# Expert sums weighed on VectorE, and added to the outputs by DMAs, in an attention and Sinkhorn-routing kernel

## The chip, the cores and the metric

The kernel runs on one core of a Trainium2 chip. The metric is device time in microseconds (us) of one execution; less is better. Three executions before the change took 891.78, 892.31 and 892.71 us, median 892.31. The profiled execution is a further one, with its own time.

A core has five engines with queues of their own. TensorE (PE in the profile) multiplies matrices, VectorE (DVE) and ScalarE (ACT) work element by element, GpSimd (POOL) can do so too and writes the descriptors of the DMAs that it issues, and SyncE (SP) here only issues DMAs. An engine runs its queue strictly in order: an instruction that waits for a semaphore holds everything behind it.

## The reference

Two blocks, one after the other. The first is a polynomial attention: queries and keys are sketched by two small projections, whose 8 x 8 outer products are the features; its result is a matrix x of 4352 tokens by 128. The second is a mixture of 8 experts, in which every token goes through every expert:

```
logits = x @ w_gate                      # 4352 x 8
P = exp(logits - max)
8 times: P /= row sums; P /= column sums; P *= N / E
for e in range(8):
    h = maximum(x @ w1[e], 0)            # 128 -> 1024
    out += P[:, e:e+1] * (h @ w2[e])     # 1024 -> 128
```

All of it is in 32-bit floats. Nearly all arithmetic is in the experts. P is positive, so a weight may be applied to x before the first product, or to the expert's result after the second.

## The kernel before, in words

Tokens lie along the free axis of the tiles and the 128 channels on the partitions: `xT` holds x transposed. The kernel avoids multiplications by fast matrix schemes: an expert's second product is computed from sums and differences of blocks of h and of w2, seven block products in place of eight, or twenty for a larger scheme, and the output is put together from four banks of PSUM by further sums.

The experts' work is cut into *groups* of tokens (list `groups`, lines 713 to 722) and *items*, one for each expert of a group. The routing weights P exist only after attention and routing are finished. To keep TensorE busy meanwhile, expert 0 is computed for all tokens and expert 1 for the first 1280, without weights, and the results are kept in SBUF: `kept[0]` (128 x 4352) and `kept[1]` (128 x 1280). These kept sums are weighed later, when P is there.

The late groups are weighted ones. Five of them have 768 tokens in three tiles of 256 columns (their first tokens are 1280, 512, 2048, 2816 and 3584; the first of them is called `PLAIN`), one has 512 tokens in two tiles and comes last. The five take experts 1 to 7, the group at 512 and the last one 2 to 7. For each of them x is multiplied by the expert's weights before the first product.

All but the first two items of the five groups are done by `middle` (line 1258). It is a planner by hand: `add(time, job)` puts jobs on a list with a planned time, the list is sorted, and the jobs are emitted in that order. So planned times only set the order in each engine's queue. A *block* is half an item, `PERIOD` = 8.83 us long (line 1255); there are 64. An item starts at t and takes two blocks, q = 0 and 1. In every block there are three slots for less urgent work (`EASE`, at 11.93, 13.85 and 16.87 from a block's start, applied one period later): `at_ease` (line 1363) moves what is in the list `soon` out and then emits a single job of the list `later`.

What the change touches:

- `weigh_half` (825): multiplies half of x (384 columns) by an expert's weights into `xe`, two items ahead. The first half takes x as it is; the second takes a negated copy of x, which `negate` (818) has ScalarE write once for each group into the free end of `hb` (`spare`).
- `copy_half` (836) and `join_halves` (843): ScalarE copies the halves to `de`, and four adding DMAs on GpSimd's queue form their sums in `de` and `xe`. The third of the four, `de[:, 0] += de[:, 1]`, waits until the first two have landed. `join_halves` is planned at t + `WEIGH` + 1, that is t + 14.49.
- `weigh_kept` (853): for group g, the i-th call loads the weights of expert i from DRAM (`pT`, broadcast over the partitions, on SP) at t + 5 and has GpSimd multiply the kept sums by them, 256 columns at a time (`weigh`, 796), with 3.7 us of plan between the pieces. One item later `plus` adds `kept[1]` to `kept[0]` by a DMA, where there are two, and for the last group `less` has GpSimd subtract one half of the columns from the other. Over all groups these are 22 multiplies of 128 x 256 and one subtraction.
- `part_of_twenty` (990): when one of a group's four banks is finished, ScalarE copies it out (`own[k]`; `evacuate`, planned at `EMPTY` in the group's last block) and a row of additions and subtractions on VectorE is put on `later`, which build the output y, three thirds of 256 columns. The first ones are: `y[:, 0]` from bank 0; `y[:, 1]` from banks 1 and 0; then, with bank 2, three operations on `y[:, 2]` and line 1011, `y[lower, 1] -= own[1][lower, 1]`, where `lower` is partitions 0 to 63. Near the end of the row three additions add the weighed kept sums to the thirds (line 1040); then the thirds are transposed and stored. The next group's first blocks carry this row, and after the fifth group the closing stage (`steps`, 1543) does.

A queue rule matters for the prediction: `keep_in_program_order` keeps GpSimd's and SP's instructions in the order in which they are emitted.

Of the kernel before, what the change touches and what calls it, by code (L numbers as in the profile page):

```python
# [10 lines left out]
F32 = mybir.dt.float32  # L11
# [39 lines left out]
def kernel(  # L51
# [736 lines left out]
    def weights_of(e, lo, n, tag):  # L788
        if tag == "pb":
            pb = spare[:, 6 * NT3 + 2 * HALF:9 * NT3 + 2 * HALF][:, 0:n]  # L790
        else:
            pb = pools[0].tile([P, 3 * NT3], F32, tag=tag, name=tag, bufs=3)[:, 0:n]
        tc.keep_in_program_order(nc.sync.dma_start(out=pb, in_=pT[e:e + 1, lo:lo + n].to_broadcast([P, n])))
        return pb

    def weigh(out, x, pb):
        tc.keep_in_program_order(nc.gpsimd.tensor_tensor(out, x, pb, op=Alu.mult))
# [15 lines left out]
    weights, turned_off = {}, {}  # L813
# [4 lines left out]
    def negate(g):  # L818

        lo = groups[g][0]  # L820
        c = 6 * NT3 + HALF * (g % 2)
        x = turned_off[g] = spare[:, c:c + HALF]
        nc.scalar.activation(out=x, in_=xT[:, lo + HALF:lo + 2 * HALF], func=Act.Copy, scale=-1.0)

    def weigh_half(j, i, engine):

        g = items[j][0]
        lo = groups[g][0]
        if i == 0:
            sources[j] = [pools[0].tile([P, 2, HALF], F32, tag="xe", name="xe", bufs=3)]  # L830
        x = turned_off[g] if i else xT[:, lo:lo + HALF]
        ins = engine.tensor_tensor(sources[j][0][:, i], x, weights[j][:, HALF * i:HALF * (i + 1)], op=Alu.mult)
        if engine is nc.gpsimd:
            tc.keep_in_program_order(ins)
# [18 lines left out]
    def weigh_kept(g, i):  # L853

        lo, n, t, es, _ = groups[g]
        ys = [kept[e][:, lo:lo + n * t] for e in range(es[0])]
        if i < len(ys):
            pb = []

            def piece(c):  # L860
                if not c:
                    pb.append(weights_of(i, lo, n * t, "pb"))
                sl = slice(c, c + NT3)
                weigh(ys[i][:, sl], ys[i][:, sl], pb[0][:, sl])

            return [lambda c=c: piece(c) for c in range(0, n * t, NT3)]

        def plus(y):
            tc.keep_in_program_order(nc.gpsimd.dma_start(out=ys[0], in_=y, accum_op=Alu.add))

        def less():
            k1, k2 = ys[0][upper, 0:n], ys[0][upper, n:2 * n]
            tc.keep_in_program_order(nc.gpsimd.tensor_tensor(k1, k1, k2, op=Alu.subtract))

        return [lambda y=y: plus(y) for y in ys[1:]] + [less] * (t == 2)
# [114 lines left out]
    def part_of_twenty(g, k):  # L990
# [7 lines left out]
        def do(out, a, b, off=False):  # L998
            at_leisure(lambda: nc.vector.tensor_tensor(out, a, b, op=Alu.subtract if off else Alu.add))
# [12 lines left out]
        if all(i in own for i in range(4)):  # L1012
# [26 lines left out]
            for i in range(3):  # L1039
                do(y[:, i], y[:, i], kept[0][:, lo + NT3 * i:lo + NT3 * (i + 1)])  # L1040
# [217 lines left out]
    def middle():  # L1258
# [114 lines left out]
        for n, k in enumerate(ks):  # L1373
# [5 lines left out]
            if q == 0:  # L1379
# [19 lines left out]
                if 1 + late <= es.index(e) <= es[0] + 1 + late:  # L1399
                    for i, do in enumerate(weigh_kept(g, es.index(e) - 1 - late)):  # L1400
                        add(t + 5 + 3.7 * i, do)
                if g == len(groups) - 2 and 3 <= es.index(e) <= 5:
                    for i, do in enumerate(weigh_kept(len(groups) - 1, es.index(e) - 3)):
                        add(t + 5 + 3.7 * i, do)
            ahead = j + 2 + q
            if new_of(ahead):
                if q:
                    add(t + WEIGH - 9, fetch_weights, ahead)
                    if items[ahead - 1][0] != items[ahead][0]:
                        add(t + WEIGH, negate, items[ahead][0])  # L1410
                add(t + WEIGH, weigh_half, ahead, 1 - q, nc.vector)
# [35 lines left out]
        add(WEIGH - 0.6, weigh_half, first_new + 2, 0, nc.vector)  # L1447
# [60 lines left out]
    def beside(j, c):  # L1508
# [17 lines left out]
        if new_of(j + 1) or new_of(j + 2):  # L1526
            for do, *a in PREPARE.get(c if new_of(j + 1) else c - 16, ()):
# [4 lines left out]
    PREPARE = {-14: ((fetch_weights, first_new),), -9: ((weigh_half, first_new, 0, nc.vector),),  # L1532
               -8: ((negate, PLAIN), (copy_half, first_new, 0)), -7: ((weigh_half, first_new, 1, nc.vector),),
               -6: ((copy_half, first_new, 1),), -5: ((join_halves, first_new),),
               0: ((fetch_weights, first_new + 1), (raw_second, first_new, "ws"), (first_weights, first_new)),
               4: ((weigh_half, first_new + 1, 0, nc.vector),), 5: ((weigh_half, first_new + 1, 1, nc.vector),),
# [194 lines left out]
```

## Time and profile before

| | |
|---|---|
| median of three runs | 892.31 us |
| profiled execution, its own time | 892.21 us |
| span of the profiled execution | 890.4 us |
| TensorE busy | 880.1 us, 99% |
| VectorE busy | 788.3 us, 89% |
| ScalarE busy | 561.7 us, 63% |
| GpSimd busy | 180.9 us, 20% |
| mean granted TensorE clock | 0.999 |

The profile gives one execution. Its groups of instructions (a row is: code line, engine, operation, output and input tiles, shape, count, then busy time in us, mean duration in ns, and the idle time before them) and its timeline (start in us, duration in us, engine, line, operation, count; in brackets the engine's idle time before it and what ended that) are used below. A source view of one line gives the shortest, median and longest duration in ns, and the first and last start in us. A windows row gives a stretch, its length, and each engine's busy time in it with its count of instructions. A DMA row gives queue, count, size in KB and the median time in us from issue to landing. Two or three equal VectorE instructions in a row are one timeline row with their joint duration. Where VectorE's instructions follow each other closely, their durations overlap a little.

### The profile page before, as it was taken

Reading aid. Unit: us, or ns where it says so; the run is one execution under the profiler, and the core shown is the slowest. Engines: PE = TensorE matmul, PEld = TensorE weight load, DVE = VectorE, ACT = ScalarE, POOL = GpSimd, SP = SyncE. Lnnn points to the kernel's source line nnn. Section 1 sums busy time; section 2 is a strip of 40 time slices with the busy share of each in tenths; the row PEclk is TensorE's granted clock in tenths of the full one; section 3 lists DMA queues with packets and bytes.
Section 4 is the critical chain, followed back from the end, with each engine's and each line's share of the span. In section 5 each row is a group of like instructions: output and inputs, shape, how many; then the busy total and the mean of one; then the engine's idle time right before and its main releaser. Section 6 shows DMA issues by size and latency. Waiting matters only on the chain.

```text
span 890.4 us, 28221 instructions
## 1 busy us (share of the span) xinstructions
PE 880.1 (99%) x11586; PEld 615.3 (69%) x11586; DVE 788.3 (89%) x1595; ACT 561.7 (63%) x1288; POOL 180.9 (20%) x242
## 2 busy tenths in 40 slices
PE   8999999999999999999999999999999999999997
PEld 6777544555677777676777777777777786666665
DVE  7678788889799999999999998999989999987865
ACT  3355477666577676676767666766667676655543
POOL 3121123012133213321222211321122213100000
PEclk9999999999999999999999999999999999999999
DMA  9996359658989777767776687567676775750340
GB/s 257 304 282 228 95 106 215 165 151 184 292 249 237 233 209 239 205 183 187 215 238 160 179 213 227 170 186 211 197 194 186 233 210 152 173 176 28 116 103 13
DMA packets 92721, 169.13 MB, mean 190 GB/s; under 512 B 28704, under 2 KB 65008, under 8 KB 87744
## 3 DMA queue, kind: packets, MB, share of 16 engines
q1 hardware_dynamic: 73264, 137.68, 49.2%
q0 software_dynamic: 18096, 29.49, 18.7%
q8 instruction: 91, 1.49, 0.7%
q10 hardware_dynamic: 1232, 0.16, 0.1%
q14 instruction: 38, 0.31, 0.1%
HBM read 123.60 MB, written 25.08 MB: 167 GB/s over the span
## 4 chain that ended last, share of the span: by engine, by line
PE 92%; DVE 5%; ACT 1%; issue 1%; DMA 1%; SPq 0%; DVEq 0%; ACTq 0%
PE s L1492 39%; PE a L1275 34%; PE a L1091 14%; PE a L423 1%; DVE hb L1177 1%; PE a L538 1%; DVE hx L1177 1%; DMA kx<-in_k_dram 1%; PE a L390 0%; DVE hb L1110 0%; PE s L452 0%; PE a L502 0%; DVE a L1312 0%; DVE hx L1312 0%; PE s L468 0%
## 5 line engine op out<-in xcount | busy, mean ns | idle before, releaser
L1275 PE MATMUL a<-xe,w 64*64 64x384 f32 x2052 | 397.4, 483 | 0.0
L1492 PE MATMUL s<-hb,ws 64*64 64x256 f32 (+4 forms) x2904 | 375.8, 384 | 1.6 <-DVE hb L1110 0.9
L1492 PE MATMUL s<-hx,ws 64*64 64x256 f32 (+1 forms) x2844 | 350.8, 377 | 0.4 <-DVE hx L1177 0.3
L1275 PE MATMUL a<-de,w 64*64 64x384 f32 x1536 | 299.2, 483 | 0.4 <-DVE a L1312 0.4
L1492 PEld LDWEIGHTS s<-hb,ws 64*64 64x64 f32 (+1 forms) x2904 | 197.0, 133 | 77.9 <-issue 30.8
L1492 PEld LDWEIGHTS s<-hx,ws 64*64 64x64 f32 (+1 forms) x2844 | 191.8, 133 | 60.9 <-issue 10.9
L1177 DVE TENSOR_TENSOR hb<-hb 128x512 f32<-128x512 f32 (+1 forms) x340 | 187.3, 576 | 3.6 <-ACT hb L1307 2.2
L1275 PEld LDWEIGHTS a<-xe,w 64*64 64x64 f32 x2052 | 139.9, 133 | 27.7 <-issue 0.9
L1307 ACT ACTIVATE hb<-a 128x384 f32<-128x384 f32 x192 | 91.5, 492 | 61.9 <-PE a L1275 57.1
L1307 ACT ACTIVATE hx<-a 128x384 f32<-128x384 f32 x192 | 91.0, 492 | 62.0 <-PE a L1275 59.2
L1177 DVE TENSOR_TENSOR hx<-hx 128x512 f32<-128x512 f32 (+1 forms) x204 | 122.9, 615 | 0.2
L1275 PEld LDWEIGHTS a<-de,w 64*64 64x64 f32 x1536 | 106.3, 133 | 22.3 <-DVE a L1312 1.5
L1091 PE MATMUL a<-xT,w 128*64 128x416 f32 (+3 forms) x512 | 119.2, 463 | 0.0
L1095 ACT ACTIVATE hb<-a 128x256 f32<-128x256 f32 (+4 forms) x152 | 68.8, 461 | 59.8 <-PE a L1091 54.0
L848 POOL DMA_DIRECT2D de<-xe x64 | 53.2, 975 | 226.2 <-PE a L1275 113.9
L1091 PE MATMUL a<-px,w 128*64 128x256 f32 (+1 forms) x512 | 93.1, 407 | 0.1
L1303 ACT ACTIVATE hb<-a 128x384 f32<-128x384 f32 x128 | 62.7, 490 | 32.5 <-PE a L1275 31.8
L1312 DVE TENSOR_TENSOR a<-a,hb 128x384 f32<-128x384 f32 x128 | 71.9, 562 | 7.3 <-PE a L1275 3.5
L1110 DVE TENSOR_TENSOR hb<-hb 128x416 f32<-128x416 f32 (+7 forms) x84 | 58.6, 698 | 21.2 <-ACT hb L1095 17.5
L1301 ACT COPY a<-a 128x384 f32<-128x384 f32 x128 | 59.3, 463 | 27.5 <-PE a L1275 26.6
L1095 ACT ACTIVATE hx<-a 128x256 f32<-128x256 f32 (+1 forms) x104 | 41.6, 400 | 42.8 <-PE a L1091 35.5
L1091 PEld LDWEIGHTS a<-xT,w 128*64 128x64 f32 x512 | 49.6, 137 | 24.6 <-issue 15.0
(217 smaller groups left out, 1034.9 us busy)
## 6 DMA issues: line engine op xcount, KB each, us to landing
ws<-ws SPq DMA_DIRECT2D x34, 1280.0 KB, 6.4
w<-wl SPq DMA_DIRECT2D x32, 512.0 KB, 8.4
w<-wf SPq DMA_DIRECT2D x32, 512.0 KB, 8.7
px<-pT SPq DMA_DIRECT2D x34, 384.0 KB, 9.3
w<-in_moe_w_dram SPq DMA_DIRECT2D x18, 512.0 KB, 4.2
de<-xe POOLq DMA_DIRECT2D x32, 192.0 KB, 3.5
de<-de POOLq DMA_DIRECT2D x32, 192.0 KB, 8.4
ph<-qa SPq DMA_DIRECT2D x12, 288.0 KB, 4.6
```

Of the source, the lines that this page charges most:

```text
L423: nc.tensor.matmul(pv[64 * s:64 * (s + 1), i], kp[0:n, H * t + h].rearrange("p i j -> p (i j)"), vx[0:n, slots[h], t, :], start=(t == 0 an ...
L848: tc.keep_in_program_order(nc.gpsimd.dma_start(out=out, in_=x, accum_op=Alu.add))
L1091: nc.tensor.matmul(ph[sl], loaded_w[j][0][:, P * f + H2 * s:P * f + H2 * (s + 1)], sources[j][:, lo:hi], start=True, stop=True, tile_posit ...
L1095: last_relu[:] = [nc.scalar.activation(out=out, in_=ph, func=Act.Relu).ins.name]
L1110: nc.vector.tensor_tensor(out, a, b, op=Alu.subtract)
L1177: nc.vector.tensor_tensor(places(out), places(a), places(b), op=Alu.subtract if off else Alu.add)
L1275: nc.tensor.matmul(out[sl], w[r, c0 + H2 * s:c0 + H2 * (s + 1)], x[r], start=start, stop=stop, tile_position=(H2 * row, H2 * s), skip_grou ...
L1301: witness(k, p, 1, nc.scalar.copy(b, bx))
L1303: witness(k, p, 5, nc.scalar.activation(out=m5s[p], in_=b, func=Act.Copy, scale=1.0 if p else -1.0))
L1307: ins = nc.scalar.activation(out=out, in_=x, func=Act.Relu)
L1312: ins = nc.vector.tensor_tensor(by if what == 1 else raw(k, p, 1, 1), bb[p], m5s[p], op=Alu.add)
L1492: mm = nc.tensor.matmul(sums[g][i][H2 * s:H2 * (s + 1), n * place:n * (place + 1)], w, x, start=c == (2 if t == 3 and row is None else 1) ...
```

## The change

Four things are changed.

1. The 22 multiplies of kept sums go from GpSimd to VectorE. Each call loads its weights at t + 5 as before, into one of two areas of `spare` by turns, and puts its pieces at t + 18 on a new list, `urgent`, which `at_ease` empties ahead of `later`, one job for a slot as before. `plus` is planned at t + 12 of the following item, `less`, now on VectorE, at two periods + 5.
2. The three additions of kept sums to y at the end of a group are gone from VectorE. In place of each, GpSimd issues an adding DMA (128 x 256, 128 KB) into a third of y, right behind the first sum (for third 2: the third sum) that VectorE writes there.
3. The negated copy of x is gone; VectorE's second half-weighing is a `scalar_tensor_tensor` that multiplies by -1 and the weights at once.
4. The areas of `spare` are laid out anew, since the negated copies no longer need theirs.

The matrix products, their order and planned times are as before.

```diff
 def weights_of(e, lo, n, tag):
-    if tag == "pb":
-        pb = spare[:, 6 * NT3 + 2 * HALF:9 * NT3 + 2 * HALF][:, 0:n]
-    else:
-        pb = pools[0].tile([P, 3 * NT3], F32, tag=tag, name=tag, bufs=3)[:, 0:n]
+    pb = pools[0].tile([P, 3 * NT3], F32, tag=tag, name=tag, bufs=3)[:, 0:n]
...
-    def negate(g):
-        ...
-        nc.scalar.activation(out=x, in_=xT[:, lo + HALF:lo + 2 * HALF], func=Act.Copy, scale=-1.0)
-
-    def weigh_half(j, i, engine):
+    def weigh_half(j, i):
...
-        x = turned_off[g] if i else xT[:, lo:lo + HALF]
-        ins = engine.tensor_tensor(sources[j][0][:, i], x, weights[j][:, HALF * i:HALF * (i + 1)], op=Alu.mult)
+        sl = slice(HALF * i, HALF * (i + 1))
+        out, x, pb = sources[j][0][:, i], xT[:, lo:][:, sl], weights[j][:, sl]
+        if i:
+            nc.vector.scalar_tensor_tensor(out, x, -1.0, pb, op0=Alu.mult, op1=Alu.mult)
+        else:
+            nc.vector.tensor_tensor(out, x, pb, op=Alu.mult)
...
-    def weigh_kept(g, i):
+    urgent = []
+
+    def weigh_kept(g, i, at_, add):
...
+        pb = spare[:, (6 + 3 * (i % 2)) * NT3:][:, 0:n * t]
+
+        def load():
+            tc.keep_in_program_order(nc.sync.dma_start(out=pb, in_=pT[i:i + 1, lo:lo + n * t].to_broadcast([P, n * t])))
+
+        def piece(c):
+            y = ys[i][:, c:c + NT3]
+            nc.vector.tensor_tensor(y, y, pb[:, c:c + NT3], op=Alu.mult)
...
         def less():
             k1, k2 = ys[0][upper, 0:n], ys[0][upper, n:2 * n]
-            tc.keep_in_program_order(nc.gpsimd.tensor_tensor(k1, k1, k2, op=Alu.subtract))
+            nc.vector.tensor_tensor(k1, k1, k2, op=Alu.subtract)
+
+        if i < len(ys):
+            add(at_ + 5, load)
+            for c in range(0, n * t, NT3):
+                add(at_ + 18 + 1e-4 * c, urgent.append, lambda c=c: piece(c))
+        else:
+            for y in ys[1:]:
+                add(at_ + 12, plus, y)
+            if t == 2:
+                add(at_ + 2 * PERIOD + 5, less)
...
-        def do(out, a, b, off=False):
-            at_leisure(lambda: nc.vector.tensor_tensor(out, a, b, op=Alu.subtract if off else Alu.add))
+        def do(out, a, b, off=False, third=None):
+            def now():
+                nc.vector.tensor_tensor(out, a, b, op=Alu.subtract if off else Alu.add)
+                if third is not None:
+                    tc.keep_in_program_order(nc.gpsimd.dma_start(
+                        out=own["y"][:, third], in_=kept[0][:, lo + NT3 * third:lo + NT3 * (third + 1)],
+                        accum_op=Alu.add))
+
+            at_leisure(now)
...
-            do(own["y"][:, 0], own[0][:, 0], own[0][:, 1])
+            do(own["y"][:, 0], own[0][:, 0], own[0][:, 1], third=0)
...
-            do(y[:, 1], own[1][:, 0], own[0][:, 0], True)
+            do(y[:, 1], own[1][:, 0], own[0][:, 0], True, 1)
...
-            do(y[lower, 2], y[lower, 2], own[2][lower, 1], True)
+            do(y[lower, 2], y[lower, 2], own[2][lower, 1], True, 2)
             do(y[lower, 1], y[lower, 1], own[1][lower, 1], True)
...
-            for i in range(3):
-                do(y[:, i], y[:, i], kept[0][:, lo + NT3 * i:lo + NT3 * (i + 1)])
...
-            if later:
-                later.pop(0)()
+            if urgent or later:
+                (urgent or later).pop(0)()
...
-                if items[ahead - 1][0] != items[ahead][0]:
-                    add(t + WEIGH, negate, items[ahead][0])
```

More of the change, by code (lines that the diff above doesn't have):

```diff
@@ L812 @@
     spare = hb[:, 25 * NT3:]
-    weights, turned_off = {}, {}
+    weights = {}
     def fetch_weights(j):
         weights[j] = weights_of(items[j][1], groups[items[j][0]][0], 3 * NT3, "px")
-    def negate(g):
-        lo = groups[g][0]
-        c = 6 * NT3 + HALF * (g % 2)
-        x = turned_off[g] = spare[:, c:c + HALF]
-        nc.scalar.activation(out=x, in_=xT[:, lo + HALF:lo + 2 * HALF], func=Act.Copy, scale=-1.0)
-    def weigh_half(j, i, engine):
+    def weigh_half(j, i):
         g = items[j][0]
@@ L851 @@
     first_new = first_weighted + 2
-    def weigh_kept(g, i):
+    urgent = []
+    def weigh_kept(g, i, at_, add):
         lo, n, t, es, _ = groups[g]
         ys = [kept[e][:, lo:lo + n * t] for e in range(es[0])]
[L857 to L866, printed above, removed]
+        pb = spare[:, (6 + 3 * (i % 2)) * NT3:][:, 0:n * t]
[4 more added lines that the diff above has]
+            nc.vector.tensor_tensor(y, y, pb[:, c:c + NT3], op=Alu.mult)
         def plus(y):
@@ L872, in less @@
             k1, k2 = ys[0][upper, 0:n], ys[0][upper, n:2 * n]
-            tc.keep_in_program_order(nc.gpsimd.tensor_tensor(k1, k1, k2, op=Alu.subtract))
-        return [lambda y=y: plus(y) for y in ys[1:]] + [less] * (t == 2)
+            nc.vector.tensor_tensor(k1, k1, k2, op=Alu.subtract)
[8 more added lines that the diff above has]
+                add(at_ + 2 * PERIOD + 5, less)
     def at_leisure(do):
@@ L1399, in middle @@
                 if 1 + late <= es.index(e) <= es[0] + 1 + late:
-                    for i, do in enumerate(weigh_kept(g, es.index(e) - 1 - late)):
-                        add(t + 5 + 3.7 * i, do)
+                    weigh_kept(g, es.index(e) - 1 - late, t, add)
                 if g == len(groups) - 2 and 3 <= es.index(e) <= 5:
-                    for i, do in enumerate(weigh_kept(len(groups) - 1, es.index(e) - 3)):
-                        add(t + 5 + 3.7 * i, do)
+                    weigh_kept(len(groups) - 1, es.index(e) - 3, t, add)
             ahead = j + 2 + q
@@ L1408, in middle @@
                     add(t + WEIGH - 9, fetch_weights, ahead)
-                    if items[ahead - 1][0] != items[ahead][0]:
-                        add(t + WEIGH, negate, items[ahead][0])
-                add(t + WEIGH, weigh_half, ahead, 1 - q, nc.vector)
+                add(t + WEIGH, weigh_half, ahead, 1 - q)
                 add(t + 13.69, copy_half, ahead, 1 - q)
@@ L1446, in middle @@
             add(at_, lambda i=i: own[i]())
-        add(WEIGH - 0.6, weigh_half, first_new + 2, 0, nc.vector)
+        add(WEIGH - 0.6, weigh_half, first_new + 2, 0)
         add(WEIGH - 0.2, copy_half, first_new + 2, 0)
```

8 lines of the change are left out of this document (3 added, 5 removed).

## The prediction

> **What bounds the kernel now.** I read the page's busy times first, then the timeline of one operation that occurs once per product and block, then the timeline of GpSimd, then VectorE around it.
>
> ```profile
> span 890.4 us, 28221 instructions
> PE 880.1 (99%) x11586; PEld 615.3 (69%) x11586; DVE 788.3 (89%) x1595; ACT 561.7 (63%) x1288; POOL 180.9 (20%) x242
> ```
>
> TensorE is busy all the time, so only a shorter chain on TensorE can shorten the kernel. The hand-written stage (`middle`) is 64 blocks, laid out by code line 1255 for one block each 8.83 us. ScalarE's seed copy (L1301) marks every block; these are the starts in blocks 2, 18, 34 and 63:
>
> ```profile
> 244.09 0.46 ACT L1301 COPY a<-a 128x384 f32<-128x384 f32 x1 [0.21 <-PE a L1275]
> ...
> 387.28 0.46 ACT L1301 COPY a<-a 128x384 f32<-128x384 f32 x1 [0.28 <-PE a L1275]
> ...
> 528.60 0.46 ACT L1301 COPY a<-a 128x384 f32<-128x384 f32 x1 [0.24 <-PE a L1275]
> ...
> 787.07 0.46 ACT L1301 COPY a<-a 128x384 f32<-128x384 f32 x1 [0.25 <-PE a L1275]
> ```
>
> Blocks 18 to 34 take 141.32 us, 16 x 8.83: the floor. The 16 blocks before take 143.19, or 1.87 too long; the 29 after take 258.47, against 29 x 8.8325 = 256.14, or 2.33 too long. So the stage loses **4.2 us** against its floor, and that is all that can be won there. Now GpSimd's multiplies of kept sums:
>
> ```profile
> L797 POOL TENSOR_TENSOR kept<-kept,hb x22: 717/1167/2273, 256.1 to 753.6; 128x256 f32<-128x256 f32 x22
> ...
> 344.19 3.36 POOL L797 TENSOR_TENSOR kept<-kept,hb 128x256 f32<-128x256 f32 x3 [9.61 <-DMA hb<-pT]
> ...
> 452.43 3.19 POOL L797 TENSOR_TENSOR kept<-kept,hb 128x256 f32<-128x256 f32 x3 [11.64 <-DMA hb<-pT]
> ...
> 575.08 3.00 POOL L797 TENSOR_TENSOR kept<-kept,hb 128x256 f32<-128x256 f32 x3 [8.89 <-DMA hb<-pT]
> ...
> 700.01 3.30 POOL L797 TENSOR_TENSOR kept<-kept,hb 128x256 f32<-128x256 f32 x3 [10.90 <-DMA hb<-pT]
> ```
>
> They come in eight bursts. At them VectorE's operations stretch, and TensorE's chain then slips:
>
> ```profile
> 344.60 2.36 DVE L1177 TENSOR_TENSOR hx<-hx 128x512 f32<-128x512 f32 x2
> ...
> 737.26 1.28 DVE L1177 TENSOR_TENSOR hx<-hx 128x512 f32<-128x512 f32 x2
> ```
>
> ```profile
> 345.12 0.85 PE a L1275 x9
> ...
> 354.38 0.85 PE a L1275 x9
> ```
>
> The same pair of subtractions takes 2.36 us inside a burst and 1.28 outside: VectorE is 1.08 late. In the chain of waits the same piece of the next block follows after 9.26 us instead of 8.83: TensorE loses 0.43. So this place forgives VectorE about 1.08 - 0.43 = 0.65 us. The burst at 452.43 lies in the stretch that lost nothing. All 4.2 us lie in the stretches that hold the other seven bursts; I put all of it to them.
>
> **The change part by part.**
>
> *The 22 multiplies leave GpSimd:* -4.2 us if nothing replaces them (from 0, if the bursts only happen to lie there, to -4.2).
>
> *They come to VectorE,* one for each slot of `at_ease`, ahead of the waiting output sums; 15 output additions of the same size go from the same slots, `less` comes in between.
>
> ```profile
> L999 DVE TENSOR_TENSOR y<-y,kept 128x256 f32<-128x256 f32 x15 | 6.1, 415 | 0.0
> ...
> L832 DVE TENSOR_TENSOR xe<-hb,px 128x384 f32<-128x384 f32 x32 | 18.0, 562 | 0.2
> ...
> L681 DVE SCALAR_TENSOR_TENSOR p<-rs,p 128x272 f32<-128x272 f32 x8 | 3.5, 442 | 0.3
> ```
>
> ```profile
> 250.00:258.80 8.80, 8.80 (x21) 1.00 1.01 304
> ```
>
> Net 22 - 15 + 1 = 8 instructions, 8 x 0.415 = 3.3 us of VectorE over 565 us of the stage. In the later groups the slots carry output sums today and the blocks still run at 8.83, so a multiply there costs 0; cover gone, at most those 3.3. In the first group VectorE has no idle time; three more instructions, 3 x 0.415 = 1.2 us, less the 0.65 forgiven, give **+0.4** to 0.6 (from 0, if queued work has slack, to 1.2). I take 0.4.
>
> *The negated copy goes:* five ScalarE activations less on an engine that is 63% busy: 0. In its place, 32 half-weighings become scalar_tensor_tensor. From 256 to 384 columns a tensor_tensor grows by 562 - 415 = 147 ns, so 272 columns would be 433; the scalar form took 442, 9 ns more, 0.3 us over 32: inside the 0.65 forgiven in each place, 0 (at most 0.3).
>
> *Weights are loaded ahead of the multiply:* the same eight loads on SP at the same places. A multiply now waits on VectorE instead of GpSimd, queued 15.8 us or more of planned time after its load (5 against 20.76 in the plan).
>
> ```profile
> hb<-pT SPq DMA_DIRECT2D x6, 384.0 KB, 9.8
> ```
>
> They land 9.8 us after issue, 6 us to spare: 0. `less` stands 10.7 us behind the adding DMA it waits for (12 against 2 periods + 5), on a GpSimd queue with nothing before it by then: 0 (at most the wait of a us or two, once). `plus` moves on GpSimd's queue from 5 to 12, still ahead of the next `join_halves`: 0.
>
> *Fifteen adding DMAs come to GpSimd's queue,* and this is what I fear. For each of five groups, thirds 0, 1 and 2 of y get `kept[0]` added by a DMA issued right behind VectorE's first sum into that third. Thirds 0 and 2 are not touched again for many slots. Third 1 is: line 1011, `y[lower, 1] -= own[1][lower, 1]`, stands four slots behind and now must wait for that DMA to land. In GpSimd's queue that DMA stands behind `join_halves` of the same item (14.49 in the plan, against slot 16.87), whose third DMA waits for the first. Where the last DMA of `join_halves` is issued, when it lands, and where line 1011 runs today, at the four group ends inside the stage:
>
> ```profile
> 333.42 1.16 POOL L848 DMA_DIRECT2D xe<-xe  x1
> ...
> xe<-xe POOLq DMA_DIRECT2D x1, 96.0 KB, 9.7
> ...
> 341.98 0.41 DVE L999 TENSOR_TENSOR y<-y,w 64x256 f32<-64x256 f32 x1
> ```
>
> ```profile
> 439.63 1.16 POOL L848 DMA_DIRECT2D xe<-xe  x1
> ...
> xe<-xe POOLq DMA_DIRECT2D x1, 96.0 KB, 11.0
> ...
> 449.44 0.41 DVE L999 TENSOR_TENSOR y<-y,w 64x256 f32<-64x256 f32 x1
> ```
>
> ```profile
> 565.02 1.17 POOL L848 DMA_DIRECT2D xe<-xe  x1
> ...
> xe<-xe POOLq DMA_DIRECT2D x1, 96.0 KB, 9.8
> ...
> 573.13 0.41 DVE L999 TENSOR_TENSOR y<-y,w 64x256 f32<-64x256 f32 x1
> ```
>
> ```profile
> 687.94 1.17 POOL L848 DMA_DIRECT2D xe<-xe  x1
> ...
> xe<-xe POOLq DMA_DIRECT2D x1, 96.0 KB, 10.2
> ...
> 697.74 0.41 DVE L999 TENSOR_TENSOR y<-y,w 64x256 f32<-64x256 f32 x1
> ```
>
> That DMA lands at 343.1, 450.6, 574.8 and 698.1. What lands later, when queued right behind it? Today's trace has one such DMA of the same 128 KB:
>
> ```profile
> 267.66 1.19 POOL L848 DMA_DIRECT2D xe<-xe  x1
> 268.19 1.62 POOL L282 DMA_DIRECT2D forms<-in_moe_w_dram  x1
> ...
> forms<-in_moe_w_dram POOLq DMA_DIRECT2D x1, 128.0 KB, 6.1
> ...
> xe<-xe POOLq DMA_DIRECT2D x1, 96.0 KB, 6.1
> ```
>
> It landed at 274.3, 0.5 us after its forerunner (273.8), on half as many partitions as ours. I take 1.0, between 0.5 and 1.5. VectorE's waits are then 344.1 - 342.0 = 2.1, 451.6 - 449.4 = 2.2, 575.8 - 573.1 = 2.7 and 699.1 - 697.7 = 1.4, in all 8.4. Behind line 1011 in VectorE's queue stand the next half-weighing, the block's subtractions and the sum L1312 that TensorE waits for; the bursts above hit this same stretch, so 0.65 is forgiven each time: 8.4 - 2.6 = **+5.8** (3.8 at 0.5, 7.8 at 1.5).
>
> The other end of that price is a DMA that isn't held back at all:
>
> ```profile
> de<-xe POOLq DMA_DIRECT2D x1, 192.0 KB, 3.1
> ```
>
> Issued at about 334.0, it would land at 337.1, five us before line 1011 needs it: 0. [...]
>
> The fifth group ends in the closing stage, with no `join_halves` before the DMA:
>
> ```profile
> 810.00:815.00 5.00, 5.00 (x50) 2.91 (x46) 3.74 (x10) 3.07 (x8) 0.00 (x0) 1.00 0.00 0
> ```
>
> A landing of 3.1 us instead of the four slots' spacing may hold VectorE a us, but it idles 1.26 of these 5: I take **+0.3** (0 to 1.3).
>
> Sum: the profiled execution took 892.21 (span 890.40, 1.81 around it), near the median 892.31. 892.2 - 4.2 + 0.4 + 5.8 + 0.3 = **894.5**.
>
> **The rivals.** *The DMA lands in time* (not slower). For it: the 3.1 row; the loads on SP that share the DMA engines may fall otherwise. Against: four landings of 9.7 to 11.0 in the very queue. It decides as soon as third 1 lands before line 1011 runs, 8.0 us after the issue of the DMA in the first case. Price: only the gain and the first group, 892.2 - 4.2 + 0.4 = 888.4.
>
> *The wait grows.* The new DMAs lengthen GpSimd's queue, and third 1 lands 2.5 us behind its forerunner instead of 1.0: 4 x 1.5 = 6.0 more, 900.5. Against: the 0.5 row.
>
> *The change doesn't do what it says:* the seven slips come from something else beside the bursts, as the adding DMAs that GpSimd writes then too; the 4.2 stays, 898.7. Against: the pair of 2.36 beside 1.28.
>
> **How the numbers follow.** Forecast 0.55 (its own range 892 to 897, from the 3.8 and 7.8 with half a us each for the small terms), landing in time 0.29, growing wait 0.10, no gain 0.06. The range reaches from just below the second, 888.0, to 898.0, which leaves out the growing wait and half of the last. A measurement of this kernel tells 0.2% from no change, 1.8 us. Below 890.5: 0.28 of landing in time and 0.01 of the rest, 0.29. Within: the lower 0.20 of the forecast and 0.01 of the second, 0.21. Above 894.1: 0.35 + 0.10 + 0.05 = 0.50.
>
> **What would show it.** Right: no stretched VectorE operations and even blocks of 8.83 at the former bursts; at four group ends VectorE idles before the 64x256 subtraction of y, released by a DMA into y, for 1.4 to 2.7 us, and that block takes 1.5 us longer. Wrong: those DMAs land within 8 us of their issue, or blocks still slip where the multiplies are; then the first or the last rival holds.

## The result and the profile after

| | before | after |
|---|---|---|
| median of the runs, us | 892.71 (7 runs, 891.78 to 892.95) | 896.91 (7 runs, 894.75 to 901.71) |
| profiled execution, us | 892.21, span 890.4 | 894.94, span 893.1 |
| ratio of the means of the runs | 1 | 1.0052 (1.0030 to 1.0074) |

The change makes the kernel half a per cent slower, and its runs lie 7 us apart where those of before lie 1.2 apart (2.0, 3.9 and 4.9 in the later sets of runs of the kernel before). In the profile after, line numbers move by a few: the seed copy is L1306, the block's subtractions are L1182, the output sums L1000 (code line 1018 is the subtraction that was line 1011), the adding DMAs L1002, `join_halves` L840. The page's first lines and its chain of waits, by engine and by line:

```profile
span 893.1 us, 28210 instructions
PE 879.1 (98%) x11586; PEld 632.3 (71%) x11586; DVE 782.9 (88%) x1603; ACT 560.5 (63%) x1283; POOL 170.2 (19%) x234
...
PE 84%; DMA 8%; DVE 6%; issue 1%; ACT 0%; SPq 0%; POOL 0%; DVEq 0%
PE s L1493 37%; PE a L1280 31%; PE a L1096 14%; DMA y<-kept 4%; DMA de<-xe 1%; DMA qx<-in_q_dram 1%; DMA kx<-in_k_dram 1%; DVE hb L1182 1%; DVE hx L1182 1%; PE a L538 1%; DMA v<-in_v_dram 1%; PE a L423 1%; DVE hb L1115 0%; DVE a L1317 0%; DVE ws L244 0%
```

VectorE and GpSimd both do less than before (788.3 and 180.9 us then), and yet the span is 2.7 us longer. The new name in the chain is the adding DMA, `y<-kept`. The seed copies of blocks 2, 18, 34 and 63, as shown of before:

```profile
243.47 0.46 ACT L1306 COPY a<-a 128x384 f32<-128x384 f32 x1 [0.21 <-PE a L1280]
...
388.40 0.46 ACT L1306 COPY a<-a 128x384 f32<-128x384 f32 x1 [0.17 <-PE a L1280]
...
531.61 0.46 ACT L1306 COPY a<-a 128x384 f32<-128x384 f32 x1 [0.24 <-PE a L1280]
...
789.64 0.46 ACT L1306 COPY a<-a 128x384 f32<-128x384 f32 x1 [0.24 <-PE a L1280]
```

The three stretches take 144.93, 143.21 and 258.03 us against floors of 141.32, 141.32 and 256.14: losses of 3.61, 1.89 and 1.89, in all 7.4 where it was 4.2. That is +3.2. The stage starts 0.62 us sooner (243.47, was 244.09; the further profiles of the kernel after have 243.90 and 243.84, so this differs from execution to execution), and what follows block 63 takes 0.13 more (893.1 - 789.64 = 103.46, was 103.33): +2.7, the difference of the spans.

Where VectorE waits in the stage, and for what (the group of that wait with total, times and longest; then the subtraction at each of the five group ends):

```profile
DVE y L1000 <- DMA y<-kept: 10.1, 5, 3.6
```

```profile
345.33 0.42 DVE L1000 TENSOR_TENSOR y<-y,w 64x256 f32<-64x256 f32 x1 [3.64 <-DMA y<-kept]
...
453.19 0.42 DVE L1000 TENSOR_TENSOR y<-y,w 64x256 f32<-64x256 f32 x1 [2.50 <-DMA y<-kept]
...
578.62 0.42 DVE L1000 TENSOR_TENSOR y<-y,w 64x256 f32<-64x256 f32 x1 [2.40 <-DMA y<-kept]
...
702.40 0.42 DVE L1000 TENSOR_TENSOR y<-y,w 64x256 f32<-64x256 f32 x1 [0.74 <-DMA y<-kept]
...
816.70 0.42 DVE L1000 TENSOR_TENSOR y<-y,w 64x256 f32<-64x256 f32 x1 [0.78 <-DMA y<-kept]
```

What one such wait does to the blocks, by the seed copies around the first of them (there are two a block; these are both of one block, the first of the next, and, with its second left out, the first of the one after that):

```profile
336.25 0.46 ACT L1306 COPY a<-a 128x384 f32<-128x384 f32 x1 [0.21 <-PE a L1280]
341.24 0.46 ACT L1306 COPY a<-a 128x384 f32<-128x384 f32 x1 [0.25 <-PE a L1280]
347.18 0.46 ACT L1306 COPY a<-a 128x384 f32<-128x384 f32 x1
...
356.89 0.46 ACT L1306 COPY a<-a 128x384 f32<-128x384 f32 x1 [0.21 <-PE a L1280]
```

From 336.25 to 356.89 are 20.64 us, against two blocks of 8.83, 17.66: the place slips by 2.98 for a wait of 3.64. Read in the same way, the four group ends slip by 2.98, 1.88, 1.77 and 0.14, in all 6.8. Almost all the rest of the 7.4 is in the first group, and the pair of subtractions that took 2.36 us inside a burst of multiplies takes 1.28 now:

```profile
347.88 1.28 DVE L1182 TENSOR_TENSOR hx<-hx 128x512 f32<-128x512 f32 x2
```

So the bursts' loss is gone, as predicted, and the wait gave back more than that.

### The profile page after: what moved, and what is told of

Its sections match the earlier page's. It is cut to its first block, busy times and chain, and to the rows that moved or that the text cites. A ratio compares the mean times of both kernels' runs of the same rounds, so it can differ in the third digit from the quotient of the medians.

```text
span 893.1 us, 28210 instructions
## 1 busy us (share of the span) xinstructions
PE 879.1 (98%) x11586; PEld 632.3 (71%) x11586; DVE 782.9 (88%) x1603; ACT 560.5 (63%) x1283; POOL 170.2 (19%) x234
## 4 chain that ended last, share of the span: by engine, by line
PE 84%; DMA 8%; DVE 6%; issue 1%; ACT 0%; SPq 0%; POOL 0%; DVEq 0%
PE s L1493 37%; PE a L1280 31%; PE a L1096 14%; DMA y<-kept 4%; DMA de<-xe 1%; DMA qx<-in_q_dram 1%; DMA kx<-in_k_dram 1%; DVE hb L1182 1%; DVE hx L1182 1%; PE a L538 1%; DMA v<-in_v_dram 1%; PE a L423 1%; DVE hb L1115 0%; DVE a L1317 0%; DVE ws L244 0%
## 5 line engine op out<-in xcount | busy, mean ns | idle before, releaser
L1493 PEld LDWEIGHTS s<-hx,ws 64*64 64x64 f32 (+1 forms) x2844 | 193.9, 133 | 53.2 <-issue 10.6
L1182 DVE TENSOR_TENSOR hb<-hb 128x512 f32<-128x512 f32 (+1 forms) x340 | 187.6, 577 | 3.3 <-ACT hb L1312 2.2
L1182 DVE TENSOR_TENSOR hx<-hx 128x512 f32<-128x512 f32 (+1 forms) x204 | 118.5, 594 | 0.2
L840 POOL DMA_DIRECT2D de<-xe x64 | 53.1, 973 | 263.8 <-ACT de L833 140.3
L1096 PE MATMUL a<-px,w 128*64 128x256 f32 (+1 forms) x512 | 96.8, 406 | 0.0
L1306 ACT COPY a<-a 128x384 f32<-128x384 f32 x128 | 59.3, 463 | 27.2 <-PE a L1280 26.5
```

The lines of the kernel that those rows point to most:

```text
L840: tc.keep_in_program_order(nc.gpsimd.dma_start(out=out, in_=x, accum_op=Alu.add))
L1096: nc.tensor.matmul(ph[sl], loaded_w[j][0][:, P * f + H2 * s:P * f + H2 * (s + 1)], sources[j][:, lo:hi], start=True, stop=True, tile_posit ...
L1182: nc.vector.tensor_tensor(places(out), places(a), places(b), op=Alu.subtract if off else Alu.add)
L1306: witness(k, p, 1, nc.scalar.copy(b, bx))
L1493: mm = nc.tensor.matmul(sums[g][i][H2 * s:H2 * (s + 1), n * place:n * (place + 1)], w, x, start=c == (2 if t == 3 and row is None else 1) ...
```

## The experiments

Two theories stood after the result; a ratio below is that of the means of the runs to the kernel before. *The wait*: the loss is VectorE standing at line 1018 for the adding DMA into third 1, and 4.2 us were really won beside it. *Contention or work*: the adding DMAs or VectorE's new multiplies cost by being there, and the wait only shows it. The kernel before ran beside each set of experiments; its medians were 892.57 (the first four), 892.27 (the next four) and 892.61 (the last two).

**e1_later: move the waiting subtraction, nothing else.** Of the kernel after; all 15 adding DMAs stay.

```diff
             do(y[lower, 2], y[lower, 2], own[2][lower, 1], True, 2)
-            do(y[lower, 1], y[lower, 1], own[1][lower, 1], True)
...
             do(e0[upper, 0], e2[upper, 1], e0[upper, 0], True)
+            do(y[lower, 1], y[lower, 1], e1[lower, 1], True)
             do(y[upper, 1], y[upper, 1], e0[upper, 0])
```

> The changed kernel with one operation moved: the subtraction of bank 1's part from third 1 of y stands further back in VectorE's row, behind the sums of the other banks, so that the adding DMA into that third has long landed. Theory (VectorE waits for that DMA): no wait of VectorE on a DMA into y in the stage; time 888 to 889.5, that is 892.2 less 4.2 us of GpSimd's multiplies plus 0.6 us of the first group; and runs within 1.5 us of each other, since the wait that differs from run to run is gone. Rival (the adding DMAs cost by their traffic, or VectorE's multiplies do): 894 to 897 as in the changed kernel.

Measured: 888.75 (4 runs, 887.62 to 889.68), ratio 0.9957 (0.9942 to 0.9972). VectorE has no wait for a DMA into y any more. The DMA itself is no quicker at the first group end (queue, size, us from issue to landing, of this kernel):

```profile
y<-kept POOLq DMA_DIRECT2D x1, 128.0 KB, 11.1
```

The same 11.1 us as in the kernel after: it lands as late, and nobody waits for it. One line moved turns +0.5% into -0.4%, so the wait is the loss and the DMAs as such cost nothing that shows. The runs lie 2.1 us apart, less than the 7 of the kernel after, but more than the 1.5 expected.

**e2_noadd: no adding DMAs.** Of the kernel after; VectorE adds `kept[0]` again, as before.

```diff
-            do(own["y"][:, 0], own[0][:, 0], own[0][:, 1], third=0)
+            do(own["y"][:, 0], own[0][:, 0], own[0][:, 1])
...
-            do(y[:, 1], own[1][:, 0], own[0][:, 0], True, 1)
+            do(y[:, 1], own[1][:, 0], own[0][:, 0], True)
...
-            do(y[lower, 2], y[lower, 2], own[2][lower, 1], True, 2)
+            do(y[lower, 2], y[lower, 2], own[2][lower, 1], True)
...
+            for i in range(3):
+                do(y[:, i], y[:, i], kept[0][:, lo + NT3 * i:lo + NT3 * (i + 1)])
```

> The changed kernel without the adding DMAs into y: VectorE adds the kept sums at the end of the row, as before the change; the multiplies stay on VectorE. Theory: 888 to 889.5, the same as with the operation moved back, since 15 additions of 0.42 us lie in slots that cost nothing. Rival (VectorE has no room for multiplies and additions both): over 890.

Measured: 888.19 (4 runs, 887.73 to 888.66), ratio 0.9951 (0.9936 to 0.9966); the stage loses 0.8. The 15 additions that the DMAs were to take from VectorE cost nothing where they stood: with 22 multiplies and 15 additions VectorE still keeps up. What the DMAs spare was hidden.

**e3_addonly: the adding DMAs alone.** Of the kernel before; the multiplies stay on GpSimd.

```diff
+        def do(out, a, b, off=False, third=None):
+            def now():
+                nc.vector.tensor_tensor(out, a, b, op=Alu.subtract if off else Alu.add)
+                if third is not None:
+                    tc.keep_in_program_order(nc.gpsimd.dma_start(
+                        out=own["y"][:, third], in_=kept[0][:, lo + NT3 * third:lo + NT3 * (third + 1)],
+                        accum_op=Alu.add))
...
-            for i in range(3):
-                do(y[:, i], y[:, i], kept[0][:, lo + NT3 * i:lo + NT3 * (i + 1)])
```

> The kernel before with the adding DMAs alone: the multiplies stay on GpSimd, the negated copy stays. Theory: the four waits of VectorE are there (0.7 to 3.6 us each), and the time is 892.7 plus 6.8, some 899, or down to 896 where a wait and GpSimd's burst behind it lie in the same place and overlap. Rival (VectorE's multiplies make the changed kernel slower): 892 to 893.

Measured: 903.93 (4 runs, 900.7 to 911.17), ratio 1.0138 (1.0082 to 1.0195). The sign and the place were right, the size was not: the stage loses 17.8 us, where the waits (3.50, 0.79, 1.85 and 2.03, less 0.65 each) and the bursts' 4.2 would make 9.8. Two things that the expectation did not have are in the trace. The waiting subtraction now runs inside a burst of multiplies, and is stretched from 0.42 to 1.50 us on top of its wait (this kernel's VectorE):

```profile
345.06 1.50 DVE L1000 TENSOR_TENSOR y<-y,w 64x256 f32<-64x256 f32 x1 [3.50 <-DMA y<-kept]
```

And TensorE, once it starts again, runs at half its clock for a while (windows of this kernel: start and end, length, busy time of PE, PEld, DVE, ACT and POOL, then the granted clock, the DMA share and GB/s):

```profile
345.00:348.00 3.00, 0.00 (x0) 0.00 (x0) 2.94 (x5) 0.90 (x3) 1.40 (x3) 1.00 0.31 44
348.00:351.00 3.00, 2.77 (x22) 1.42 (x26) 3.00 (x6) 0.95 (x2) 1.57 (x2) 0.50 0.55 84
351.00:354.00 3.00, 3.00 (x50) 2.32 (x46) 2.09 (x6) 1.14 (x3) 0.44 (x1) 0.93 0.12 19
```

In the three microseconds at clock 0.50 TensorE ran 22 matmuls, in the next three 50. The clock was halved behind two of the four stops, for 3.4 us each time (at the fourth end the two windows of 3 us from 713.00 have 0.54 and 0.89). At the third end it stayed full, and two VectorE instructions inside the burst took 0.95 and 2.33 us in place of 0.41 each, 2.5 us more together; there the place slips 3.70, which is its wait of 1.85 less 0.65, and 2.5. At the fourth end both come together. So a stop of TensorE can cost more than its length here, and so can a wait that moves VectorE's work into a burst.

**e4_nomult: no multiplies on GpSimd, nothing in their place.** Of the kernel before, without the weighting of the kept sums.

```diff
-                weigh(ys[i][:, sl], ys[i][:, sl], pb[0][:, sl])
```

> The kernel before without GpSimd's 22 multiplies of the kept sums; it leaves the weighting of the kept sums of experts 0 and 1 out. Theory (the multiplies stretch VectorE's operations): every block of the stage 8.83 us, time 888 to 888.8. Rival (the blocks slip at these places for another reason, as the loads of weights): 892 to 893.

Measured: 888.0 (4 runs, 887.6 to 888.86), ratio 0.995 (0.9935 to 0.9965). The stage loses 0.3 in place of 4.2, and the pair of subtractions beside the former burst is short again:

```profile
344.69 1.29 DVE L1176 TENSOR_TENSOR hx<-hx 128x512 f32<-128x512 f32 x2
```

So GpSimd's bursts cost 892.57 - 888.0 = 4.6 us. e2 pays for the same products on VectorE and lies 0.2 above: there they are all but free.

**e5_order: the DMA ahead of `join_halves` in GpSimd's queue.** The prediction held that queue's order to be what makes the DMA late. Of the kernel after, at group ends only:

```diff
-                    add(t + WEIGH + 1, join_halves, ahead)
+                    add(t + WEIGH + (3.9 if g > PLAIN and es.index(e) == 0 else 1), join_halves, ahead)
```

> The changed kernel with one planned time moved: in the first item of each later group join_halves is planned 2.9 us later, so that the adding DMA into third 1 stands ahead of it in GpSimd's queue; the row of VectorE stays as it is. Theory (that DMA lands late because it stands behind the four DMAs of join_halves): it lands 3 to 5 us after VectorE's first sum into third 1, VectorE waits for it at no group end of the stage, time 888 to 890. Rival (an adding DMA into y takes 10 us there wherever it stands, from the loads that share the DMA engines): the waits stay, 894 or more. A third outcome: de and xe come 2.9 us later and TensorE waits for them instead.

Measured: 888.54 (5 runs, 888.19 to 889.24), ratio 0.996 (0.9946 to 0.9975): the waits in the stage are gone. But the DMA, though first in its queue, did not land in the 3 to 5 us expected. Its issue, its landing, and the subtraction, of the first group end of this kernel:

```profile
331.97 0.88 POOL L1002 DMA_DIRECT2D y<-kept  x1 [6.58 <-PE a L1280]
...
y<-kept POOLq DMA_DIRECT2D x1, 128.0 KB, 8.1
...
341.46 0.41 DVE L1000 TENSOR_TENSOR y<-y,w 64x256 f32<-64x256 f32 x1
```

It landed at 331.97 + 8.1 = 340.1, 1.4 us before the subtraction. At the other three ends it took 9.9, 10.4 and 10.1 us from its issue, little less than in the kernel after (10.8, 10.8 and 10.1). The third of them, and the subtraction there:

```profile
560.88 0.85 POOL L1002 DMA_DIRECT2D y<-kept  x1 [5.75 <-PE a L1280]
...
y<-kept POOLq DMA_DIRECT2D x1, 128.0 KB, 10.4
...
571.31 0.42 DVE L1000 TENSOR_TENSOR y<-y,w 64x256 f32<-64x256 f32 x1
```

It landed 0.03 us ahead of the subtraction here, and 0.5 and 0.2 ahead at the second and fourth end. Set against the block's seed copy, the DMA was issued 2.1, 2.1, 1.9 and 1.0 us sooner than in the kernel after, and landed 5.1, 3.0, 2.4 and 1.0 sooner. So the queue's order is worth 1 to 5 us, at three ends just enough to end the wait; the eight to ten that are left are not its doing. In that time the DMA engines are full (window of this kernel, columns as above):

```profile
332.00:340.00 8.00, 8.00 (x132) 5.81 (x128) 7.83 (x18) 5.33 (x13) 2.56 (x3) 1.00 0.97 292
```

In the kernel after, the same DMA was seen in both surroundings: at the first group end, and in the closing stage with idle DMA engines (windows and landings of the kernel after):

```profile
333.00:345.00 12.00, 11.98 (x186) 8.03 (x177) 8.54 (x18) 7.50 (x17) 3.49 (x4) 1.00 0.96 292
807.00:812.00 5.00, 5.00 (x56) 2.98 (x52) 3.22 (x8) 3.19 (x8) 0.55 (x1) 1.00 0.01 3
```

```profile
y<-kept POOLq DMA_DIRECT2D x1, 128.0 KB, 11.1
...
y<-kept POOLq DMA_DIRECT2D x3, 128.0 KB, 2.6
```

2.6 us at a DMA share of 0.01, 11.1 at 0.96. That SP's loads are what fills the engines is read from the trace (in the kernel after, from 333 to 346 us, its queue has 62% of the engines' time, GpSimd's 26%); that they are what makes the landing late is argued from these rows, as a kernel without those loads was not tried.

**e6_both: e1, and the first group's multiplies moved.** To see whether the remaining loss of e1, all in the first group, goes too:

```diff
-                late = 2 if g == PLAIN else 0
+                late = 5 if g == PLAIN else 0
```

> The changed kernel with the subtraction moved back, as before, and the three multiplies of the first group put at its last item, where VectorE makes no second weights. Theory (these three cost 0.6 us where VectorE has no idle time): no slip in the fifth and sixth block, 0.6 us less than with the subtraction moved alone, 887.5 to 888.5. Rival (the slip comes from elsewhere): the same as with the subtraction moved alone, and the slip is still there.

Measured: 888.21 (6 runs, 887.65 to 889.0), ratio 0.9956 (0.9944 to 0.9969). Two seed copies of the first group, in the kernel after, then in e6, one block apart each:

```profile
270.06 0.46 ACT L1306 COPY a<-a 128x384 f32<-128x384 f32 x1 [0.25 <-PE a L1280]
...
279.44 0.46 ACT L1306 COPY a<-a 128x384 f32<-128x384 f32 x1 [0.27 <-PE a L1280]
```

```profile
270.63 0.46 ACT L1306 COPY a<-a 128x384 f32<-128x384 f32 x1 [0.21 <-PE a L1280]
...
279.46 0.46 ACT L1306 COPY a<-a 128x384 f32<-128x384 f32 x1 [0.21 <-PE a L1280]
```

9.38 us became 8.83: the slip there is gone and the stage loses 0.1 in all. By the clock e6 is 0.5 below e1, which the spread of either (1.4 and 2.1) can't tell from nothing. e1, e2, e5 and e6 all beat both kernels.

**e7_sooner: a longer wait, nothing else.** If the wait sets the price, a longer one must cost more. Of the kernel after, the subtraction one slot earlier:

```diff
-            do(y[lower, 2], y[lower, 2], own[2][lower, 1], True, 2)
             do(y[lower, 1], y[lower, 1], own[1][lower, 1], True)
+            do(y[lower, 2], y[lower, 2], own[2][lower, 1], True, 2)
```

> The changed kernel with the waiting subtraction one slot earlier in VectorE's row (ahead of the third operation on third 2), which makes each of the four waits some 2.2 us longer: 5.8, 4.7, 4.6 and 2.9 us. If a wait costs its length less 0.65 and no more: the changed kernel's profiled 894.9 plus 8.8, 903 to 905. [...] Rival (the waits hide elsewhere): 895 to 897.

Measured: 913.7 (4 runs, 910.52 to 914.94), ratio 1.0236 (1.0215 to 1.0257), above both numbers. In its profile VectorE waits (total, times, longest)

```profile
DVE y L1000 <- DMA y<-kept: 18.3, 5, 5.8
```

of which 5.81, 4.40, 3.98 and 2.83 at the four group ends of the stage. Less 0.65 each, that would be 14.4 us of slip. The blocks slip by 8.26, 6.8, 3.6 and 2.4, in all 21.1: 3.1 and 3.0 more at the first two, 0.3 and 0.2 more at the others. The clock tells these apart (windows of this kernel: the stop at the first end, what follows it, what follows that, and what follows the third end's stop):

```profile
341.70:346.70 5.00, 0.00 (x0) 0.00 (x0) 0.89 (x3) 0.87 (x2) 0.00 (x0) 0.91 0.55 144
346.80:352.40 5.60, 5.60 (x48) 3.60 (x52) 4.05 (x10) 1.79 (x4) 0.85 (x1) 0.50 0.16 23
352.60:356.00 3.40, 3.40 (x56) 2.46 (x52) 2.29 (x5) 1.36 (x3) 1.59 (x2) 0.99 0.56 88
589.70:593.00 3.30, 3.30 (x56) 2.54 (x60) 3.30 (x9) 1.79 (x4) 0.86 (x1) 1.00 0.02 3
```

48 matmuls in 5.6 us at half clock, 56 in 3.4 at full. Behind the stop TensorE has some 6 us at half clock, and half of that is the 3 us that the first end (and likewise the second) lost beyond its wait; at the third end the clock stayed full and only 0.3 was lost beyond it.

**after_again and after_third: the kernel after, twice more.** Not edited; to see why its runs lie so far apart.

> The changed kernel once more, for a second profile. If its runs differ (894.8 to 901.7) because the adding DMA lands at other times: a time above 895.5 comes with waits of VectorE on DMAs into y longer than the 9.3 us in the stage of the first profile, and above 898 with a window of granted clock 0.5 behind one of them. Rival (the runs differ for another reason): the waits are the same as in the first profile whatever the time.

> The changed kernel a third time. If the time goes with VectorE's waits on the adding DMAs: waits of some 10 us in all at 895, some 12 at 899, with a window of granted clock 0.5 behind a wait at 898 and above and none below 895.5. Rival: a time and waits that do not go together.

Measured: 898.86 and 894.83. The wait's group in the one and in the other:

```profile
DVE y L1000 <- DMA y<-kept: 12.1, 5, 4.0
```

```profile
DVE y L1000 <- DMA y<-kept: 9.6, 5, 3.9
```

With the first profile's 10.1 at 894.94, three executions of one kernel stand in the order of their waits: the adding DMA, issued among full DMA engines (a share of 0.96 in the first profile), did not hold VectorE equally long each time (at the fourth group end 0.74 us in the first profile, 2.46 and 0.65 in these two). The 12.1 has more to it. Its first wait was 3.95, 0.31 above the 3.64 of the first profile, but the place slipped 4.86 in place of 2.98. The windows behind that stop, first in the profile of the first execution, then in that of 898.86:

```profile
347.50:350.90 3.40, 3.40 (x52) 2.21 (x56) 3.40 (x7) 0.95 (x3) 1.23 (x2) 1.00 0.58 89
```

```profile
349.30:352.60 3.30, 3.30 (x31) 2.33 (x27) 3.30 (x7) 0.25 (x1) 0.20 (x2) 0.51 0.50 80
```

31 matmuls in place of 52. Half of 3.4 us is 1.7, and the slip exceeds its wait less 0.65 by 4.86 - 3.30 = 1.56. Of the 2.0 us that the waits grew in all, 1.7 are at the fourth group end, 2.46 in place of 0.74. So the tail of this kernel's runs has two parts, longer waits and a clock halved behind one of them. That every run above 898 had it is not shown, as only profiled executions have windows; their mean granted clocks (0.996 for 901.71 and 0.997 for 898.23, against 1.000 for 894.75 and 894.94) fit it: in the kept traces whose clock is halved at the very end alone, when TensorE is done, the mean is 0.998 or more.

**e8_scalar: the negated copy alone.** Of the kernel before, to test a term put at zero:

```diff
-        x = turned_off[g] if i else xT[:, lo:lo + HALF]
-        ins = engine.tensor_tensor(sources[j][0][:, i], x, weights[j][:, HALF * i:HALF * (i + 1)], op=Alu.mult)
...
+        sl = slice(HALF * i, HALF * (i + 1))
+        out, x, pb = sources[j][0][:, i], xT[:, lo:][:, sl], weights[j][:, sl]
+        if i:
+            nc.vector.scalar_tensor_tensor(out, x, -1.0, pb, op0=Alu.mult, op1=Alu.mult)
+        else:
+            nc.vector.tensor_tensor(out, x, pb, op=Alu.mult)
...
-                    if items[ahead - 1][0] != items[ahead][0]:
-                        add(t + WEIGH, negate, items[ahead][0])
```

> The kernel before without the negated copy alone: VectorE's second half-weighing is the scalar_tensor_tensor, multiplies and additions stay where they were. Theory (five ScalarE activations less and 9 ns more on 32 VectorE instructions are hidden): 892 to 893, the slips at GpSimd's bursts as before. Rival (the form or the lost copy matters): off by more than 1 us either way.

Measured: 892.28 (10 runs, 890.33 to 893.15), ratio 0.999 (0.9978 to 1.0002): no difference that can be told. The groups of the two forms in this kernel (busy time and mean ns of one):

```profile
L834 DVE SCALAR_TENSOR_TENSOR xe<-xT,px 128x384 f32<-128x384 f32 x32 | 17.6, 549 | 0.2
...
L836 DVE TENSOR_TENSOR xe<-xT,px 128x384 f32<-128x384 f32 x32 | 17.8, 557 | 6.1 <-PE a L1277 5.6
```

## Why the prediction came out as it did

The profiled execution was forecast at 894.5 and took 894.94, with waits at the four places named. The terms, in us:

| term | forecast | in the profiles | shown by |
|---|---|---|---|
| multiplies leave GpSimd | -4.2 | -4.2 in the stage (-4.6 by the medians) | e4; even blocks there in the kernel after |
| first group | +0.4 | +0.6 | the 9.38 block; e6 takes it away |
| waits at line 1011 | +5.8 | +6.8 | slips beside the waits; e1 takes them away, e7 makes them longer |
| closing stage | +0.3 | +0.1 | 103.46 against 103.33 |
| scalar form, negated copy | 0 | 0 | e8 |
| the 15 additions gone, 22 multiplies come | 0 beside the first group | 0 | e2 beside e4 |
| all that precedes block 2 | not in the sum | -0.6 | its seed copy at 243.47, was 244.09 |

-4.2 + 0.6 + 6.8 + 0.1 - 0.6 is 2.7, the difference of the two profiled executions. The last -0.6 was in no term, and the start of the stage scatters by about as much: 242.96 to 244.13 in the kept profiles of the kernel after and its variants, 243.59 to 244.51 in those of the kernel before and its variants. Without it the profiled execution would have come to some 895.5; that the measured 894.94 lies within 0.5 of the forecast is partly luck.

**The bursts.** All 4.2 us of loss was put to seven bursts of multiplies by one stretched pair of instructions. That held: without them (e4) the stage ran to within 0.3 of its floor. The rival in which the 4.2 stays fell with it. The 0.4 of the first group was a choice out of 0.4 to 0.6; the 0.6 that 3 x 0.415 less 0.65 gives is what was measured.

**The forgiven 0.65.** It came from one burst: late by 1.08, slipped by 0.43. At the four group ends the waits less the slips are 3.64 - 2.98, 2.50 - 1.88, 2.40 - 1.77 and 0.74 - 0.14: 0.66, 0.62, 0.63 and 0.60. It is a property of the place and carries over from one cause of lateness to another.

**The landing 1.0 us behind its forerunner** is the term that was mis-sized. At the first end `join_halves` and the adding DMA stood in GpSimd's queue, and landed, like this (issues, then landings, of the kernel after):

```profile
333.68 1.17 POOL L840 DMA_DIRECT2D xe<-xe  x1
334.22 1.54 POOL L1002 DMA_DIRECT2D y<-kept  x1
```

```profile
y<-kept POOLq DMA_DIRECT2D x1, 128.0 KB, 11.1
...
xe<-xe POOLq DMA_DIRECT2D x1, 96.0 KB, 10.0
```

334.22 + 11.1 = 345.3 and 333.68 + 10.0 = 343.7: 1.6 us apart, and 2.4, 2.2 and 1.8 at the next ends, when worked out alike. That is nearer to the 2.5 of the rival in which the wait grows than to the 1.0 taken from one row of before, and outside its bounds of 0.5 to 1.5. It did not bring that rival's 900.5, because a second error went the other way: the forerunners landed sooner against line 1018 than against line 1011 before. From readiness to the forerunner's landing (343.7 less 345.33 - 3.64, and so on) it is 2.0, 0.0, 0.1 and -1.1 us, where the trace of before gave 1.1, 1.2, 1.7 and 0.4. The DMA's delays sum to 4.0 more than forecast, the leads to 3.4 less, and the four waits came to 9.3 in place of 8.4. The +6.8 against +5.8 is partly right by that luck. Of the four waits, forecast at 1.4 to 2.7 each, two lie outside, 3.64 and 0.74; the place, the releaser and the sum were right, the single waits were not.

**The reason given for the late landing** was the queue: the DMA stands behind `join_halves`. e5 put it ahead, and it still took 8.1 to 10.4 us. The queue's order moved the landing by 1 to 5 us, enough to decide this wait, but the bulk of the ten goes with full DMA engines (a share of 0.97 there), whoever stands ahead. The rival "lands in time" was weighed with this same queue as what spoke against it, and SP's loads only as something that may fall otherwise; the time that it named, 888.4, is what e1 (888.75) and e5 (888.54) take by removing the wait in two ways.

**The median,** 896.91, lies 2.4 above the forecast. The sum was made for one execution and took waits for a fixed number. The runs showed that these waits differ from execution to execution, and that in one of them, 898.86, the clock was halved behind the longest wait (0.51 in that window); neither had a term.

## What to carry to other kernels

Work that is moved from a busy engine to a DMA is still on the path when an instruction of that engine touches the same tile soon after (here four waits, 9.3 us in all): look for the next reader or writer of what the DMA writes, price the landing by DMAs at the DMA share of that very stretch (here 2.6 us at 0.01, 11.1 at 0.96), and move the reader some slots down its queue if it comes too early. And price the moved work where it stands now: here the 15 additions on the engine that was 89% busy were free, and the 22 multiplies on the one that was 20% busy cost 4 us through the other's stretched instructions.

## What the runs showed of the hardware beside that

**TensorE's granted clock was halved behind some stops, and not by their length.** By the idle time ahead of the restarting matmul (the profile models the end of the one before), TensorE stood for 2.44 us in the first profile of the kernel after, and the clock stayed full; for 2.74 in that of 898.86, and it was halved; for 3.31 at the third group end of e7, and it stayed full. The traces also hold the times at which the granted clock changed. These lie whole multiples of 3.413 us apart: in e7 it changed after 341.33, 6.83, 105.81, 6.83 and 443.73 us, which are 100, 2, 31, 2 and 130 of them; in the first profiles of the kernels before and after, where it was full until TensorE was done, after 884.05 and 887.47, which are 259 and 260. Here is the 898.86 execution in two such intervals, and e7 in the two that its third stop touches (columns as above; a DMA share over 1 comes from packets that end behind the interval):

```profile
345.96:349.37 3.41, 1.22 (x20) 0.76 (x24) 3.31 (x8) 1.67 (x4) 1.58 (x2) 1.00 0.12 18
349.38:352.79 3.41, 3.41 (x34) 2.44 (x30) 3.31 (x7) 0.17 (x1) 0.31 (x2) 0.50 0.47 75
```

```profile
584.77:588.18 3.41, 1.58 (x24) 0.71 (x16) 0.00 (x0) 1.94 (x5) 0.00 (x0) 1.00 1.06 349
588.18:591.59 3.41, 1.93 (x32) 1.49 (x36) 2.87 (x7) 0.59 (x2) 0.09 (x1) 1.00 0.07 29
```

The stop of 2.74 left one interval with 2.19 us of idle time, and the next ran at half clock. The longer stop of e7 was split, 1.83 and 1.48, and nothing happened. All five halvings behind a stop in the kept traces follow an interval that was idle for 2.19 to 3.41 us (2.19 in the 898.86 execution, 2.84 and 3.16 in e3, 2.56 and 3.41 in e7), and no interval of full clock that was idle for 1.83 or less was followed by one; what holds between these two was not measured. In e7 the interval behind each of its two halvings was itself idle for 0.91 and 1.16 us, and the clock stayed at half for one more: that is the 6.83. What makes the clock change at these times was not shown. In these traces, then, where a stop falls counts beside its length: behind stops of 2.74 (898.86), 3.27 and 3.38 us (both e3) the clock was halved, behind stops of 2.67 (after_third), 3.10 (e3) and 3.31 (e7) it was not, and two executions of one kernel, 894.94 and 898.86, differ by it.

**The scalar form was no slower** than the plain product at this size, 549 against 557 ns in e8; the 9 ns more that the prediction took from another shape weren't there.
